# A fused attention and gMLP block: the first loads held one behind another, `wo` loaded earlier, and a new instruction order

## The chip, the cores and the metric

One core of a Trainium2 chip runs the kernel. The time is device microseconds of that core, the median of several executions. One further execution is taken by the hardware profiler; its own time is given beside its span, since a profiled execution is a little longer than the others. The engines are called PE (TensorE, matmul), DVE (VectorE), ACT (ScalarE), POOL (GpSimd) and SP (SyncE, which here only issues transfers).

## The reference

Two blocks with a residual each, on x of 2048 tokens by 512 channels (one batch, bf16).

```python
def _layernorm(x, axis=-1, eps=1e-05):
    m = jnp.mean(x, axis=axis, keepdims=True)
    v = jnp.var(x, axis=axis, keepdims=True)
    return (x - m) / jnp.sqrt(v + eps)

def _A_ref(x, wqkv, wo):                      # linear attention, 32 heads of 16
    qkv = (x @ wqkv).reshape(B, S, 3, H, Dh).transpose(2, 0, 3, 1, 4)
    q, k, v = qkv[0], qkv[1], qkv[2]
    phi = lambda t: jnp.where(t > 0, t + 1, jnp.exp(t)) + 1e-06
    pq, pk = phi(q), phi(k)
    kv = jnp.einsum('bhsd,bhse->bhde', pk, v)
    z = jnp.einsum('bhsd->bhd', pk)
    num = jnp.einsum('bhqd,bhde->bhqe', pq, kv)
    den = jnp.einsum('bhqd,bhd->bhq', pq, z)[..., None] + 1e-06
    return (num / den).transpose(0, 2, 1, 3).reshape(B, S, D) @ wo

def _B_ref(x, w_in, w_sp, b_sp, w_out):       # gMLP, 2 * 896 hidden channels
    z = gelu(x @ w_in)
    z1, z2 = z[..., :Fh], _layernorm(z[..., Fh:])
    g = jnp.einsum('ts,bsf->btf', w_sp, z2) + b_sp[None, :, None]
    return (z1 * g) @ w_out

h = x + _A_ref(_layernorm(x), A_wqkv, A_wo)
out = h + _B_ref(_layernorm(h), B_w_in, B_w_sp, B_b_sp, B_w_out)
```

## The kernel before

Tokens are cut into 16 tiles of 128. The kernel records 853 operations, each with the memory that it reads and writes, through `g.add` (line 106); helpers such as `matmuls` (394), `act` (409 to 423), `dve`, `pool`, `dma` (432) and `dma_t` (a transposing transfer, 435) do so, which is why most rows of the profile carry a helper's line. The order in which the operations are issued is written into the kernel as one packed list, `ORDER` (line 16). `schedule` (144) unpacks it and gives every engine its part of the list in that order; `emit` (163) puts a semaphore wait before an operation wherever it needs something from another engine or from a transfer. Each engine works through its list strictly in order. The estimates `cost` and `lat` of an operation serve the planner's start times, which in the kernel itself only sort an operation's waits.

Stages, in the order of the work of PE:

- **Head.** x is loaded as four single tiles (0 and 2 by SP, 1 and 3 by ACT) and six pairs. The K part of `wqkv` comes in two halves, `wk0` (SP) and `wk2` (ACT), the Q part as `wq`. The pairs are held by SP until tile 0 has landed (`behind`, which adds a dependency, line 481). A warm-up of 42 small matmuls (593) runs while x is on its way. Per tile: `bn_stats` and `bn_aggr` (510, 511) on DVE, the reciprocal root on ACT or POOL (516 to 529; tile 1's moments on ACT and POOL, 534 to 550), the norm (555 on DVE, or ACT), and the transpose to channels by tokens, `xnT`: for tiles 0 to 5 on PE (569) with an eviction by ACT, for the others by a transposing transfer of SP.
- **K and Q.** Per tile four matmuls with K (`psum<-wqkv,xnT`), the map phi (`e` on ACT; 581 and 586 on DVE), and four matmuls that sum pk and xn into four banks (649): the sum over tokens of x's norm times pk, from which kv follows with V's weights. The Q products (`psum<-xnT,wqkv`) stand between them.
- **Joint.** The four sums are copied to `ct`, `wv` is applied (714), the result is masked by heads (`kvm`, 718), multiplied with `wo` and copied to `m` (four products, ACT evictions). So q times m is the attention's output. The denominators (745) go through a log and an exp on ACT to `rcp`, and SP spreads them over partitions (`r<-rcp`, 736); DVE scales pqT with them (758).
- **h.** Per tile four matmuls `psum<-m,pqT`, h by DVE (770), its moments by ACT (`sh`) and POOL (542 to 550), the norm `hn`, and a transposing transfer to `hnT`.
- **gMLP.** Two products with `w_in`: `win2` (796, 799; z2, per tile) and `win1` (`psum<-hnT,win`; z1T, per 512 tokens); z2's norm; the product with `w_sp`, which SP loads with transposing transfers (`wsp`); the gate (864, 865); the product with `w_out` (`wout`), the sum with h (855) and the output.

The loads behind the head are all issued by SP, in the order of the packed list: after the ten xnT transposes come win1, wout, wv, two wsp, win2, a wsp and wo, then the transfers of r and, between them, those of hnT.

Of the kernel before, what the change touches and what calls it, by code (L numbers as in the profile page):

```python
# [8 lines left out]
ACT = mybir.ActivationFunctionType  # L9
ALU = mybir.AluOpType  # L10

P = 128
GRAN = 16
EARLY = 1
SEM_NS = 45.0
ORDER = "c-jTQ13(x66a>(_`&;u?tD)6uwc1+qs)en!Ev*`Bwr$(CZQHhO+qSLuGQbJW$b`(uf~;^wHn_nN8Q}tVc)$~32thG~!W%gO5QbDpiDXEN<VXz%2tM#dF62fIc%eAL;fE3^g}i8hMreq}$c{YlM+8bE9}1u(@*@(3P!Iu#LNv;wA}XLTDj^U>5QHXZie^Ye5}Knjs-Y;VpgMxl0x^g~RkT74)I=@RQCGA?Yjj38bU}CYKri$}U-UyfVo?U8k$|ySirT1yaj1(iD2sAvgSM!L`WS%T=!14Rgu_^jC0K^`=z#G^hY6U3<(P;xNRJgrfmK+EshEuZ7>;2Wh}9T@wHSoK7>Q9hfR5;dX_$f;n2wp4g@c%nd02oWIErI9juSYA*%*SMSc7#qiPLzF7kGlYs;6hDucug#4cLf<ScGlZj!oE%Ihc#x*n=I|iCs90GuVrL*pDsPip#iyb2yI+xPgnfgsZrTYq*YAc#SuBiCegb+qi?fxQ}FffaG-GTcqPdq-O@c!y`P#4}8aae85L!=4X7uSNz34{KOZ0Ln@|VYNlisW+j-GY4{6%%t&WC(uvvVPB*$T6Z5bz!|1{yEXHv9vjl%5fMRh*Ffa2lKMSxR$v-d#GKfVP%#tj{(u`yj<5-r}8P5=wqX)ColeJigp<K*njAm`tU@V)nD|66`i@1adEYCWu$)#+`R&31{?7`K{NpHr`hrZ0kp6tfWtiZag$BL}PL?*EpmvK4ka|LsAGRx3cLpYpO*?<jMnN!%ETeyZpIf6~th`F_uxipM^s={i_BY%x#Z}wpuwq-lEXJ7W?DE8-Qc3@LB<}~J2KIK<I70@=0;aC<{Ax&iw?dBeKWM>ZI0Pf{<1}IQL3RY2tDnwx#%uejWfh?wQ6<35xXa-B_G$U0?XBeeel~%OMC_yob(_!9byvphb@35RM^EJ!s3Xk#)uktasb0%kT9LIAucW@5paw5-i9`|uS7jP}t@f`2+9@q0cH*h2G^DW=;J$Lc|5Aqr}@en6*J}0n&8fqac=n0>)qAKYDA95v+@fk1hIIr^rKhQ^w)L2c_RL#^}E!0x2)LL!SR_)YY9n?{s^qYzL!_WM}ul&m-rB!96Qx$#WbDrck{^Ke>B1C=XMc&{|{@_o(;7fkuDJD~LImlhvRaLu~LMe5Nm-vg-lwKL+C=Yomhf*oEBriEBqrBy!>dK_d%A!}yDwDI)D5qSNO*K?Y)8(eV>ZyL}rGc8EL7Jr@>Z~qWsjeEX{+g^Q8m7S-sj(WW5gMme8lX8EuRfZl_3EbX>aDe!sZr{oxtgz<s;vc@s(Bi%2^yn`nytlJrw!Vqjhdt-TB^-js4ZHf)mo&jTBdDUt`*v@9Xg^t+N*s!s{J~kV>+mvI;7(|r}Mg?UAm~<I;m4Stuwlzo4Tdjx~wa@s%v_ycY379dZN3!r~CS-WcEqP?VG+Rm8Gy(dal=cp_lru_xdac`=Ouut6%!65BjH+_C~O*_FI3H+A<qWW|qd%nxmyNCrfWx%+=g1qdk?od02MKW*O{(oXy2DnWyD2FDqgJ=4ZZ^$MRbN%VoLE-wIlw6|%e*Y#|nEK^A7-meYJJ!Ae<KD`%xG(u!NSm9X*_W3g7oqAbGVtfE!2L`$-VI-zIEXT|K23foy-S5Z5xXuG45R>9(}vi%1tWsrd"


class _Op:
# [13 lines left out]
class _Prog:  # L33
# [219 lines left out]
def bass_sequential_preLN__linear_attn_block__mixer_gmlp__prompt_kernel(  # L253
# [11 lines left out]
    _, S, D = A_x.shape  # L265
# [4 lines left out]
    NT, KD, KF = S // P, D // P, FH // P  # L270
# [7 lines left out]
    g = _Prog(nc)  # L278
# [37 lines left out]
    TB, SB = HT * GW * 2, HT * P * 2  # L316
# [26 lines left out]
    m = g.sbuf("m", o_m, [KD, D], BF16)  # L343
# [43 lines left out]
    def pair(b):  # L387
        return psum[:, b:b + 2, :]
# [42 lines left out]
    def dma(eng, out_ap, in_ap, name, issue=100.0, lat=2500.0, **k):  # L431
        return g.add(eng, lambda q: q.dma_start(out_ap, in_ap), [in_ap], [out_ap], cost=issue, lat=lat, dma=name, **k)  # L432
# [36 lines left out]
    wq = A_wqkv.rearrange("(c p) f -> p c f", p=P)  # L469
    queue = {"SP": [], "ACT": []}  # L470

    def load(eng, dst, src, nm, lat, issue=500.0):
        return dma(eng, dst, src.rearrange("(c p) f -> p c f", p=P), nm, lat=lat, issue=issue)

    def first_load(eng, dst, src, nm, lat, behind=None):
        q = queue[eng]
        op = load(eng, dst, src, nm, lat)
        op.bias = 1e6
        if q:
            op.soft.add(q[-1].i)  # L480
        if behind is not None:
            op.deps.add(behind.i)
        q.append(op)
        return op

    def load_x(eng, n, w, lat, behind=None):
        return first_load(eng, x[:, n:n + w, :], x_d[n * P:(n + w) * P, :], f"x{n}", lat, behind)

    x0 = load_x("SP", 0, 1, 2150)
    load_x("ACT", 1, 1, 2250)  # L490
    load_x("SP", 2, 1, 2500)
    load_x("ACT", 3, 1, 2500)
    for eng, c in (("SP", 0), ("ACT", 2)):
        first_load(eng, wqkv[:, c:c + 2, D:2 * D], A_wqkv[c * P:(c + 2) * P, D:2 * D], f"wk{c}", 3600)
    for n, lat in ((4, 2400), (6, 2600), (8, 2800), (10, 3000), (12, 3200), (14, 3400)):
        load_x("SP", n, 2, lat, x0)
    first_load("SP", wqkv[:, :, 0:D], A_wqkv[:, 0:D], "wq", 4600)
    exp_table = g.add("ACT", lambda ac: ac.preload_act_table_set("natural_log_exp_and_others"), [], [], cost=1300)
    exp_table.soft.add(queue["ACT"][-1].i)
    exps = []  # L500
# [101 lines left out]
    def next_pair():  # L602
        pc[0] += 1
        return PAIRS[pc[0] % 2]
# [83 lines left out]
    qs = [(tg, c) for tg in range(NG) for c in range(0, KD, 2)]  # L688
# [7 lines left out]
    for dst, src, nm in ((wqkv[:, :, 2 * D:3 * D], A_wqkv[:, 2 * D:3 * D], "wv"), (wo, A_wo, "wo"),  # L696
                         (win2, B_w_in[:, FH:F], "win2"), (win1, B_w_in[:, 0:FH], "win1"),
                         (wout, B_w_out, "wout")):
        late = load("SP", dst, src, nm, 2000, issue=src.shape[0] * src.shape[1] * 2 / 350)
        late.soft.add(g.last.i)  # L700


# [18 lines left out]
    for c in range(KD):  # L721
        b = CB[1 - c % 2]
# [15 lines left out]
    for tg in range(NG):  # L738
# [12 lines left out]
        if tg not in MERGE:  # L751
# [38 lines left out]
    for n in range(NT):  # L790
        b = next_pair()
# [11 lines left out]
        src = pair(b).rearrange("p a b -> p (a b)")[:, 0:FH]  # L803
        s = st3[:, n, :]
# [145 lines left out]
```

## Time and profile before

| | us |
|---|---|
| median of 7 executions | 236.38 (236.24 to 238.67) |
| profiled execution, its own time | 237.69 |
| its span, first to last instruction | 236.0 |
| PE busy | 228.7 (97%) |
| DVE busy | 147.4 (62%) |
| ACT busy | 97.5 (41%) |
| POOL busy | 46.1 (20%) |
| transfers | 23.67 MB, mean 100 GB/s |

The mean granted clock of PE over the span is 0.993. A row of the profile names the line, the engine, the operation and what it writes and reads; the times of the queries count from the start of the span. A wait is put down to what ended it last. The rows of a queue (SPq, ACTq) are the issuing of transfers, not the transfers themselves: how long one took is given as the time from issue to landing. The chain goes back from the last instruction and names at each step what released it.

### The profile page before, as it was taken

To read this page: it belongs to the slowest core of one execution; us is meant where nothing else is said; L and a number is where in the kernel's file an instruction comes from. 1 tells how busy PE (TensorE), PEld (TensorE's weight loads), DVE (VectorE), ACT (ScalarE), POOL (GpSimd) and SP (SyncE) were. 2 spreads that over 40 slices of the span, in tenths; PEclk is the share of its full clock that TensorE was granted. 3 is DMA by queue.
4 is the path that set the end of the run, shared out by engine and by line. 5 is a ranking of instruction groups with operands and counts; after the bars stand their busy time and mean duration, and the time that the engine had idled before them with its cause. 6 is when DMAs were issued, how large, how long until landed. Compare 5 with 4: busy or idle time off the path is not lost.

```text
span 236.0 us, 3061 instructions
## 1 busy us (share of the span) xinstructions
PE 228.7 (97%) x1141; PEld 106.0 (45%) x1141; DVE 147.4 (62%) x275; ACT 97.5 (41%) x172; POOL 46.1 (20%) x134
## 2 busy tenths in 40 slices
PE   7899999997999999999999999999999999999995
PEld 6444444452434444454444444444444444444452
DVE  3799765645897430723699796686665018967373
ACT  5576664486999777669761000210001000010000
POOL 3443220000456442226881000000000000000000
PEclk9799999999999999999999999999999999999999
DMA  6982317999344332369999970000000000002044
GB/s 193 292 182 46 74 26 218 261 256 262 89 74 107 67 67 47 67 154 187 139 226 246 198 171 0 0 0 0 3 0 0 0 0 3 0 0 68 0 155 137
DMA packets 58863, 23.67 MB, mean 100 GB/s; under 512 B 48480, under 2 KB 58720, under 8 KB 58848
## 3 DMA queue, kind: packets, MB, share of 16 engines
q1 hardware_dynamic: 58144, 22.88, 43.3%
q10 hardware_dynamic: 704, 0.59, 0.8%
q8 instruction: 9, 0.15, 0.3%
q14 instruction: 6, 0.05, 0.1%
HBM read 7.47 MB, written 2.10 MB: 41 GB/s over the span
## 4 chain that ended last, share of the span: by engine, by line
PE 79%; SPq 6%; DMA 5%; ACT 3%; DVE 3%; POOL 2%; issue 1%
PE psum L402 66%; PE psum L796 5%; SPq L435 4%; PE psum L649 4%; PE psum L799 4%; DMA wo<-in_A_wo_dram 3%; DMA x<-in_A_x_dram 1%; DMA r<-rcp 1%; ACT e L421 1%; DVE h L770 1%; SPq L432 1%; ACT m L421 1%; POOL st L536 1%; DVE pqT L758 1%; POOL rs L550 1%
## 5 line engine op out<-in xcount | busy, mean ns | idle before, releaser
L402 PE MATMUL psum<-wsp,z 128*128 128x512 bf16 x208 | 46.9, 379 | 0.0
L421 ACT ACTIVATE psum<-psum 128x512 f32<-128x512 f32 x12 | 7.0, 583 | 85.3 <-DVE u L864 50.5
L402 PEld LDWEIGHTS psum<-wsp,z 128*128 128x128 bf16 x208 | 20.3, 98 | 24.6 <-DVE z L555 0.2
L864 DVE TENSOR_TENSOR u<-psum,bsp 128x512 bf16<-128x512 f32 x16 | 11.1, 691 | 27.4 <-PE psum L402 27.3
L402 PE MATMUL psum<-hnT,win 128*128 128x512 bf16 x112 | 26.0, 379 | 0.0
L402 PE MATMUL psum<-wout,z1T 128*128 128x512 bf16 (+1 forms) x119 | 25.2, 367 | 0.0
L402 PE MATMUL psum<-t,s 128*128 128x512 bf16 x96 | 22.2, 379 | 0.0
L421 ACT ACTIVATE e<-psum 128x1024 bf16<-128x1024 f32 (+1 forms) x18 | 16.7, 927 | 12.4 <-PE psum L402 12.1
L421 ACT ACTIVATE z1T<-psum 128x512 bf16<-128x512 f32 x28 | 16.2, 595 | 4.8 <-PE psum L402 4.8
L402 PEld LDWEIGHTS psum<-wout,z1T 128*128 128x128 bf16 x119 | 11.6, 98 | 12.8 <-DVE z1T L865 0.5
L421 ACT ACTIVATE z<-psum 128x896 bf16<-128x896 f32 x16 | 14.6, 913 | 5.0 <-PE psum L799 4.9
L402 PE MATMUL psum<-wqkv,xnT 128*128 128x512 bf16 x64 | 16.5, 409 | 0.0
L796 PE MATMUL psum<-win,hnT 128*128 128x512 bf16 x64 | 16.4, 379 | 0.0
L402 PEld LDWEIGHTS psum<-hnT,win 128*128 128x128 bf16 x112 | 10.1, 98 | 13.3 <-ACT z1T L421 3.5
L649 PE MATMUL psum<-pk,xn 128*128 128x512 bf16 x64 | 15.3, 380 | 0.0
L402 PE MATMUL psum<-m,pqT 128*128 128x512 bf16 x64 | 15.0, 380 | 0.3 <-DVE h L770 0.2
L402 PE MATMUL psum<-xnT,wqkv 128*128 128x512 bf16 x64 | 15.3, 379 | 0.0
L855 DVE TENSOR_TENSOR h<-psum,h 128x512 bf16<-128x512 f32 (+1 forms) x17 | 10.8, 657 | 6.9 <-PE psum L402 6.9
L402 PEld LDWEIGHTS psum<-t,s 128*128 128x128 bf16 x96 | 9.4, 98 | 11.3
L812 DVE BATCH_NORM_STATS2 st<-z 128x6 f32<-128x512 bf16 x9 | 6.2, 687 | 12.0 <-ACT z L421 11.9
L799 PE MATMUL psum<-win,hnT 128*128 128x384 bf16 x64 | 13.0, 326 | 0.0
L770 DVE SCALAR_TENSOR_TENSOR h<-psum,x 128x512 bf16<-128x512 f32 x16 | 10.8, 687 | 3.1 <-PE psum L402 3.0
(99 smaller groups left out, 307.4 us busy)
## 6 DMA issues: line engine op xcount, KB each, us to landing
r<-rcp SPq DMA_DIRECT2D x16, 128.0 KB, 2.8
out_dram<-h SPq DMA_DIRECT2D x15, 128.0 KB, 1.8
win<-in_B_w_in_dram SPq DMA_DIRECT2D x2, 896.0 KB, 5.5
x<-in_A_x_dram SPq DMA_DIRECT2D x6, 256.0 KB, 5.7
wqkv<-in_A_wqkv_dram SPq DMA_DIRECT2D x2, 512.0 KB, 8.2
wout<-in_B_w_out_dram SPq DMA_DIRECT2D x1, 896.0 KB, 8.5
wo<-in_A_wo_dram SPq DMA_DIRECT2D x1, 512.0 KB, 6.6
bsp<-in_B_b_sp_dram SPq DMA_DIRECT2D x1, 512.0 KB, 4.4
```

The costliest lines, as they stand in the source:

```text
L402: inst = pe.matmul(out_ap, lhsT=a, rhs=b, start=start and i == 0, stop=stop and i == len(pairs) - 1, **kw)
L421: return g.add("ACT", lambda ac: ac.activation(out_ap, in_ap, func, **kw), [in_ap, *extra], [out_ap] + ([accum] if accum is not None else []),
L432: return g.add(eng, lambda q: q.dma_start(out_ap, in_ap), [in_ap], [out_ap], cost=issue, lat=lat, dma=name, **k)
L435: return g.add("SP", lambda q: q.dma_start_transpose(out_ap, in_ap), [in_ap], [out_ap], cost=issue, lat=lat, dma=name, **k)
L536: pool(lambda p: p.tensor_scalar(ve, s[:, 2:3], s[:, 1:2], EPS_LN, op0=ALU.add, op1=ALU.add), [s[:, 1:3]], [ve], 240)
L649: inst = pe.matmul(bank(CB[c]), lhsT=xn[:, i, c * P:(c + 1) * P], rhs=pk[:, i, :], start=i == 0, stop=i == NT - 1)
L770: dve(lambda v, n=n, b=b, s=s: v.scalar_tensor_tensor(h[:, n, :], bank(b), 1.0, x[:, n, :], op0=ALU.mult, op1=ALU.add, accum_out=s[:, 0:1] ...
L796: pe.matmul(bank(b), lhsT=hnT[:, c, n * P:(n + 1) * P], rhs=win2[:, c, 0:GW], start=c == 0, stop=c == KD - 1)
L799: inst = pe.matmul(bank(b + 1, F2), lhsT=hnT[:, c, n * P:(n + 1) * P], rhs=win2[:, c, GW:FH], start=c == 0, stop=c == KD - 1)
L812: dve(lambda v, n=n, s=s: v.bn_stats(s[:, 0:6], z2[:, n, 0:GW]), [z2[:, n, 0:GW]], [s[:, 0:6]], GW)
L855: dve(lambda v, o=o, b=b: v.tensor_tensor(o, bank(b, w), o, ALU.add), [bank(b, w), o], [o], w, ps=True)
L864: dve(lambda v: v.tensor_tensor(t, bank(b), add, ALU.add), [bank(b), add], [t], GW, ps=True)
```

## The change

Three edits. The first pair of tiles, 4 and 5, is loaded with no wait. Pair 6 waits for tile 0, pair 8 for tile 2, and pairs 10, 12 and 14 for `wk0`. The estimates of latencies for the planner are set anew, among them 5500 in place of 2000 for the late weights. The packed list is a new one of the same 853 operations. On SP, the loads behind the head come as follows: nine xnT transposes, wo, the tenth, win2, wout, win1, a wsp, wv, a wsp, the transfers of r. Of the later wsp transposes of 8 blocks, two stand among the hnT transposes of tiles 4 to 7, five ahead of the last four hnT, and the rest behind. On PE, the products of the head are laced differently (transposes and K products of single tiles in turn), the second denominator product comes ahead of the product with wv, and a Q product comes between the two halves of the products with wo. The order of DVE, ACT and POOL follows.

```diff
-ORDER = "c-jTQ13(x66a>...
+ORDER = "c-jTQ13(x66a>...
...
     x0 = load_x("SP", 0, 1, 2150)
     load_x("ACT", 1, 1, 2250)
-    load_x("SP", 2, 1, 2500)
+    x2 = load_x("SP", 2, 1, 2500)
     load_x("ACT", 3, 1, 2500)
-    for eng, c in (("SP", 0), ("ACT", 2)):
-        first_load(eng, wqkv[:, c:c + 2, D:2 * D], A_wqkv[c * P:(c + 2) * P, D:2 * D], f"wk{c}", 3600)
-    for n, lat in ((4, 2400), (6, 2600), (8, 2800), (10, 3000), (12, 3200), (14, 3400)):
-        load_x("SP", n, 2, lat, x0)
-    first_load("SP", wqkv[:, :, 0:D], A_wqkv[:, 0:D], "wq", 4600)
+    wk = [first_load(eng, wqkv[:, c:c + 2, D:2 * D], A_wqkv[c * P:(c + 2) * P, D:2 * D], f"wk{c}", 3500)
+          for eng, c in (("SP", 0), ("ACT", 2))]
+    for n, lat, behind in ((4, 3900, None), (6, 3500, x0), (8, 3600, x2), (10, 3300, wk[0]), (12, 3500, wk[0]),
+                           (14, 3700, wk[0])):
+        load_x("SP", n, 2, lat, behind)
+    first_load("SP", wqkv[:, :, 0:D], A_wqkv[:, 0:D], "wq", 4500)
...
-        late = load("SP", dst, src, nm, 2000, issue=src.shape[0] * src.shape[1] * 2 / 350)
+        late = load("SP", dst, src, nm, 5500, issue=src.shape[0] * src.shape[1] * 2 / 350)
```

The instruction order of SP around the late loads, before and after:

```
before                                   after
xnT transposes x10                       xnT transposes x9
win1                                     wo
wout                                     xnT transpose x1
wv                                       win2
wsp x2                                   wout
win2                                     win1
wsp                                      wsp
wo                                       wv
r transfers x12                          wsp
                                         r transfers x12
```

More of the change, by code (lines that the diff above doesn't have):

```diff
@@ L15 @@
 SEM_NS = 45.0
-ORDER = "c-jTQ13(x66a>(_`&;u?tD)6uwc1+qs)en!Ev*`Bwr$(CZQHhO+qSLuGQbJW$b`(uf~;^wHn_nN8Q}tVc)$~32thG~!W%gO5QbDpiDXEN<VXz%2tM#dF62fIc%eAL;fE3^g}i8hMreq}$c{YlM+8bE9}1u(@*@(3P!Iu#LNv;wA}XLTDj^U>5QHXZie^Ye5}Knjs-Y;VpgMxl0x^g~RkT74)I=@RQCGA?Yjj38bU}CYKri$}U-UyfVo?U8k$|ySirT1yaj1(iD2sAvgSM!L`WS%T=!14Rgu_^jC0K^`=z#G^hY6U3<(P;xNRJgrfmK+EshEuZ7>;2Wh}9T@wHSoK7>Q9hfR5;dX_$f;n2wp4g@c%nd02oWIErI9juSYA*%*SMSc7#qiPLzF7kGlYs;6hDucug#4cLf<ScGlZj!oE%Ihc#x*n=I|iCs90GuVrL*pDsPip#iyb2yI+xPgnfgsZrTYq*YAc#SuBiCegb+qi?fxQ}FffaG-GTcqPdq-O@c!y`P#4}8aae85L!=4X7uSNz34{KOZ0Ln@|VYNlisW+j-GY4{6%%t&WC(uvvVPB*$T6Z5bz!|1{yEXHv9vjl%5fMRh*Ffa2lKMSxR$v-d#GKfVP%#tj{(u`yj<5-r}8P5=wqX)ColeJigp<K*njAm`tU@V)nD|66`i@1adEYCWu$)#+`R&31{?7`K{NpHr`hrZ0kp6tfWtiZag$BL}PL?*EpmvK4ka|LsAGRx3cLpYpO*?<jMnN!%ETeyZpIf6~th`F_uxipM^s={i_BY%x#Z}wpuwq-lEXJ7W?DE8-Qc3@LB<}~J2KIK<I70@=0;aC<{Ax&iw?dBeKWM>ZI0Pf{<1}IQL3RY2tDnwx#%uejWfh?wQ6<35xXa-B_G$U0?XBeeel~%OMC_yob(_!9byvphb@35RM^EJ!s3Xk#)uktasb0%kT9LIAucW@5paw5-i9`|uS7jP}t@f`2+9@q0cH*h2G^DW=;J$Lc|5Aqr}@en6*J}0n&8fqac=n0>)qAKYDA95v+@fk1hIIr^rKhQ^w)L2c_RL#^}E!0x2)LL!SR_)YY9n?{s^qYzL!_WM}ul&m-rB!96Qx$#WbDrck{^Ke>B1C=XMc&{|{@_o(;7fkuDJD~LImlhvRaLu~LMe5Nm-vg-lwKL+C=Yomhf*oEBriEBqrBy!>dK_d%A!}yDwDI)D5qSNO*K?Y)8(eV>ZyL}rGc8EL7Jr@>Z~qWsjeEX{+g^Q8m7S-sj(WW5gMme8lX8EuRfZl_3EbX>aDe!sZr{oxtgz<s;vc@s(Bi%2^yn`nytlJrw!Vqjhdt-TB^-js4ZHf)mo&jTBdDUt`*v@9Xg^t+N*s!s{J~kV>+mvI;7(|r}Mg?UAm~<I;m4Stuwlzo4Tdjx~wa@s%v_ycY379dZN3!r~CS-WcEqP?VG+Rm8Gy(dal=cp_lru_xdac`=Ouut6%!65BjH+_C~O*_FI3H+A<qWW|qd%nxmyNCrfWx%+=g1qdk?od02MKW*O{(oXy2DnWyD2FDqgJ=4ZZ^$MRbN%VoLE-wIlw6|%e*Y#|nEK^A7-meYJJ!Ae<KD`%xG(u!NSm9X*_W3g7oqAbGVtfE!2L`$-VI-zIEXT|K23foy-S5Z5xXuG45R>9(}vi%1tWsrd"
@@ new lines @@
+ORDER = "c-jTQ13(x66a>(_`&;u?tD)6uwc1+qs)en!Ev*`Bwr$(CZQHhO+qSLuGQbJW$b`(uf~@d>CmfLxE^tQ}LQo8$00=`eq(myDMshen@J0^ggcp3^i(JSJKNLqeN}xRQq9RJ60xF>a8X-IKz#kDPfP5&4D3nGa<VPe5A{qfGjK*k)L?odJnxYw+qX;S^27#!CAXGt7R7DF^M@`f~Ewn-$x}q~;(FNU52Cm2kH`Gx}v_@@=MLZHv2X!$HqcH}Hu@p<N48bUia%h9L=#CWVfu87v@tA-~n26;_i!@k)RY-@GNRQs=gTCm8dZ>^77=U(Yj}AD1gE)l4n2O05h(Q>PBRGm<IF8{MhSeB>kr;)wIE87Lf{y5f8JLdwn1`8IfD>4QbvTWuIEiO?f#;~JCzyrV7=oeLfc032Mc9b#*oIBmj5(N#-PnU2*oj>@i!<1Zeb|pJ*orH-jB_}T3%G%cxP+^?iEFryS9pWhc!^uMi#xc7+jxLvypQB`U^+fTdS>8Tyu%|r#&>+gd;GvBe85+HMrQuQU;M-ue8X?lQ);GUDyCo-W~CDy>CB8w%QXCjKk#E77G@a3=}#ACViA_0E8XbMY|P7i%+CTW$T$`w7(lT&BS^+GkU=cUU>d8lENih4LztcA=)q8Waxt5+23s<LIq1dmtjUrr#nOyq6r)+2br{R8T+LQ&&K~rkFJoASIqA(sT*5V6%FS%eE!@fqtjM~o$NFr*N^HnPCec^BnM-@vf=#%VJz1H#S(Ulih?AK|>)4G`IGnjPghM%kZP=FW*q+PSft}f%z34ALHDwjnS7SC%HRe}d^=2RTWk2@k0Pf{J?&lyDP+{d$L5*Y~711;XC`i*8sG<s1s6tdsGZ>~}EUu|M%y32M2#>OaN~$9Vaxgow3rBG@4{!`;au#QEERS&;xAQnpa1PgV0}pZ>=W;nuasf|sJSTD<OR2OX6|E@6Dn@ZCqce<Gf^PFN%jyoVu$;>4Dqr(4-|z{4^ADf$E>H0+&+!@?s*xJ2iJEEx=W`(^@gDE<IydqLAMhdH@*UsvJRfldFYqFt@e&X5FaHsG&XwH37ktT`yvbW!#a-OQ52QY_k}Bvk6ID@3N~<rdtglR`WJ<3La#V6T=o`ONswQ_iDWg&-rBdk!v&%!C${{cPWNI~2bG49<TB?;=tBu;Ko!YB|I;xYZ%SD-#S<cF$ta`;yOe1f(Dw}f3<fbaBrK+l-n)=1b>Z_jWr(Wu>l^Uq&8l>8qp&^>3&KjmJ>Z;)yp(&cC!5XQl8ml=Ps&QJQRT{6knx}5+uHNdQ0h+JHnyIxKr3LDv(VDF>nxKiAq$OIfb=siSTBxPkq-ENu&Dx?x+Ny0@t`*v@9Xg^t+N*s!s{J~kgF2?2I;7(|sZ%<wGuoxyI;Zoxpv$_VtGcKgx~W^brrWx!d%CYjdaNh<sJD8j4@zdAl-#~3g?&>hd!^@ktv7n1m-?=!dauuNu%G&?ulk{XN@>3Y`>h8`ZD}pD(bActrLjMfnWeW3=48&6#azwBGFm2cx9nEL@>_rvFgNqCtmbLiEQfiSpZQuI3$|PqV!6%V@>-~cSwRc5AoI4I=3@y~+{#)x3%3#$W3g7o%3C2TWu-0BA}r1-S|v-gC`+>II-xttXU}w4MeUM`*+Uh!v#MYvE#9K7vi%3_(U5@"
```

## The prediction

> **What bounds the kernel now.** I read the busy times first, then TensorE's (PE's) waits, then the chain, and last the time lines around each place where PE lost time. The page's first part:
>
> ```profile
> PE 228.7 (97%) x1141; PEld 106.0 (45%) x1141; DVE 147.4 (62%) x275; ACT 97.5 (41%) x172; POOL 46.1 (20%) x134
> ```
>
> PE is busy for all but 7.3 us of the span of 236.0 us, and both kernels issue the same matmuls, so a reordering can win only idle time or half-rate time, and it loses by making new idle time. The waits of PE say where the idle time lies:
>
> ```profile
> PE psum L569 <- DVE xn L555: 1.5, 3, 1.0
> PE psum L402 <- DMA wo<-in_A_wo_dram: 1.4, 1, 1.4
> PE psum L593 <- POOL warm L439: 1.0, 1, 1.0
> ```
>
> (Total us, times, longest.) Three losses: the first tiles' norm (1.5), `wo` (1.4), and the constant that the warm-up reads (1.0, before any input has landed); the other two rows are 0.2 each. The chain and PE's time line around the third:
>
> ```profile
> 48.79 6.61 DMA wo<-in_A_wo_dram
> 55.40 0.14 issue
> 55.54 0.39 PE psum L402
> ```
> ```profile
> 55.54 0.59 PE L402 MATMUL psum<-wo,kvm 128*128 128x512 bf16 x2 [1.38 <-DMA wo<-in_A_wo_dram]
> 56.06 0.40 PE L745 MATMUL psum<-pqT,zc 128*32 128x512 bf16 x4
> 56.60 0.88 PE L402 MATMUL psum<-wo,kvm 128*128 128x512 bf16 x2
> 57.32 1.89 PE L402 MATMUL psum<-xnT,wqkv 128*128 128x512 bf16 x8
> 59.04 1.24 PE L402 MATMUL psum<-m,pqT 128*128 128x512 bf16 x5
> ```
>
> `wo` is the last load of SP's queue, issued at 48.79, landed at 55.40. The table by stretch shows the rest:
>
> ```profile
> 7.93:11.35 3.42, 3.42 (x12) 1.45 (x12) 3.02 (x9) 1.74 (x4) 1.24 (x3) 0.50 0.97 292
> ...
> 50.00:59.00 9.00, 7.38 (x52) 3.23 (x49) 4.23 (x7) 6.72 (x12) 0.00 (x0) 1.00 1.01 265
> 59.00:67.00 8.00, 7.58 (x38) 3.25 (x38) 6.85 (x18) 7.56 (x15) 4.45 (x11) 1.00 0.37 82
> 67.00:77.00 10.00, 9.89 (x49) 4.38 (x48) 8.36 (x23) 9.86 (x25) 5.41 (x15) 1.00 0.52 93
> ```
>
> (Columns: length; busy PE, weight loads, DVE, ACT, POOL; granted clock; DMA share; GB/s.) One stretch of 3.4 us in the head runs at half clock: eight matmuls step by 0.43 us there against 0.22 after it, 1.6 us lost while PE counts as busy. From 59 to 77 ACT and DVE are nearly full as well, so time gained ahead of 59 may be given back there.
>
> **Part 1, wo first.** SP's order behind the xnT transposes was win1, wout, wv, wsp, wsp, win2, wsp, wo. It becomes wo (ahead of the last xnT transpose), then that transpose, win2, wout, win1, wsp, wv, wsp. wo is issued at about 30.6 (the transpose that now stands last but one is ready near 29: its norm on ACT moves up ahead of two exps). It costs 0.58 us of SP; the last transpose, whose norm ends near 33.4, goes out near 33.5 (35.19 before), so SP waits there anyway and wo is hidden. wo lands near 35 and is out of the question.
>
> What follows on PE is then set by kvm. The q product and r product (50.07 to 51.3), the wv product of 16 matmuls (1.06, 51.3 to 52.4), a q product (0.86, to 53.2), which covers DVE's kvm (0.69, done at 53.1). Two wo products (0.43), q (0.86) to 54.5. The first two m evictions on ACT (0.6 each) follow its rcp, which ends at 53.74, so they end near 54.9; two wo products to 55.1; the r product 0.4; two q products 1.73 to 57.2. ACT has e (1.03) and two m (1.1) to do after 54.8, to 56.9. So the first m,pqT product starts near 57.2 where it started at 59.04: -1.8 us. ACT's own hole, 53.74 to 55.95, goes with it, so its full stretch starts earlier too.
>
> Given back: the products 4 and 5 wait for PSUM evictions, which DVE (0.69 each) makes in line with the r scalings: 0.45 and 0.2. r lands sooner: it was issued at 51.57 and took 4.1 to 4.7 us behind wo, against 2.8 as the median of all r transfers; the first scaling, at 57.02 before, can start near 55.4. Products 8 and 14 wait 0.4 each for the scalings of the third and fourth groups, where before gaps of 0.2 to 0.4 stood at like places. I count 0.6 lost of the 1.8: **-1.2 us** after 77.
>
> **Part 2, wv late.** wv moves behind 2.7 MB of other weights. Before, win1 landed 5.1 us after its issue, wout 4.0 us later (at 45.6), wv at 47.0 (9.3 us after its issue). SP's own time line has the order, and two wsp issues held 4.6 and 3.9 us by the full queue:
>
> ```profile
> 36.50 0.58 SPq L432 DMA_DIRECT2D win<-in_B_w_in_dram  x1
> 37.13 0.50 SPq L432 DMA_DIRECT2D wout<-in_B_w_out_dram  x1
> 37.67 0.56 SPq L432 DMA_DIRECT2D wqkv<-in_A_wqkv_dram  x1
> 38.28 8.56 SPq L435 DMA_TRANSPOSE wsp<-in_B_w_sp_dram  x2
> 46.89 0.58 SPq L432 DMA_DIRECT2D win<-in_B_w_in_dram  x1
> ```
>
> Now: win2 issued near 34.75, landed 39.9; wout 43.9; win1 47.2 to 47.9; wsp 0.9; wv 1.4 more: 49.5 to 50.2. Needed at 51.3. The row bounds it from above by the transfer that stood behind two wsp before (win2, 52.8, a stall of 1.5), from below by nothing (0). I take 0, since bytes and start are counted, and keep 1.5 for the range.
>
> **Part 3, the head.** x4 goes out at 2.2 instead of 3.56. It stands in SP's queue behind wk0, and it landed at 7.39 before, with wk0 at 6.68 and wk2 (ACT's queue) at 6.89, while the DMA engines moved 302 GB/s from 4.5 to 7.9 at a share of 0.93: it is rate-bound, and lands at 7.0 to 7.4. [...] By the row, where x4's first pieces had landed at 6.30, ahead of the end of both weights, they shared the engines already, and the cost is 0. I take 0 and keep 0.4: the first k product can't start before 7.3, when its xnT eviction ends.
>
> Wait for wk0: the load of x10 now holds SP from 4.6 to 6.7, with x12, x14, wq, the first wsp and all xnT transposes behind it. They go out from 6.7 to 8.8 instead of 5.0 to 7.0. The queue doesn't run dry: x8 landed only at 10.1. The wsp issue, held until 13.44 by the queue before (6.38 us; 1.3 to 2.9 where free), ends near 13.5 again, at worst at 8.8 + 6.4 = 15.2. The first xnT transpose waits for its norm on ACT, now near 14.7 (two evictions and an exp moved ahead), and lands near 17.2 to 18; its product comes at 18.9.
>
> PE's order: transpose 0, 2, k0, transpose 1, k2, and so on. k0 starts near 7.3 (8.16 before), half of it ahead of the half-rate stretch; transpose 1 waits for tile 1's norm, which is 0.7 later (8.5), since one stats of x4 (0.69) and an ACT step (0.28) stand ahead. Then 0.43 us a matmul to 11.35, k3 to 13.0, the rest set by DVE's pk: the k product of tile 6 starts near 18.9 against 19.07, and the product after it has no 0.2 us hole: **-0.3 us**, between -0.9 and +0.8.
>
> [...] Row: 1.91 of 3.41 us busy from 4.52 to 7.93, and half rate in the next. By the row the stretch stays (0). [...]
>
> **Part 4, from 77 to the end.** wsp transposes move between the hnT transposes: two by 80, then five ahead of the last four hnT. Two cost 2.6 us of SP; hnT 5 is then issued near 80 and lands near 82.5, needed at 85. The five: 1.31 us each where the queue was empty (98.9 to 101.6), 1.64 as the mean of nine back to back; so 6.6 to 8.2 us from 89, four hnT of 1.27, and 2.5 to land: 103 to 105, needed near 107.9. No cost. Nothing in the tail moves the last product or its output (2.5 us behind PE's end). 0, with +0.5 for small holes, since PE had none from 75.4 to 233.
>
> **Sum:** -1.2 - 0.3 = -1.5: span 234.5. The profiled execution took 237.69 (span 236.0 and 1.7 around it), so it would take 236.2; the runs' median is 236.38, and the same step from it gives **234.9 us**. From no change a measurement of this kernel tells about 0.5%, or 1.2 us.
>
> **Rivals.** (a) ACT and DVE take the gain: they are 9.9 and 8.4 busy of 10 us from 67 to 77. For it: that row; against: ACT's hole at 54 closes too. Time 236.2. (b) wv is late by 1.5: the same wait under another name; 236.4. For it the 8.5 and 9.3 us that wout and wv took; against it the start, 1.75 us sooner. (c) Slower: the five wsp ahead of the last four hnT are held by a full queue as from 38.28 to 46.84 (3.9 and 4.6 us each) instead of 1.3 to 1.6. It decides from 2.2 us each; at 2.9 it cancels the gain and costs 2 more: 238.4. Against it: wsp are alone in the queue there. [...]
>
> **Numbers.** Forecast 0.52, (a) 0.20, (b) 0.10, (c) 0.09, (d) 0.09. The forecast's own range is 233.7 to 235.6; faster by over 0.5% means below 235.2. The forecast gives 0.46 faster and 0.06 same; (a) 0.04, 0.14, 0.02; (b) 0, 0.07, 0.03; (c) all slower; (d) 0.01, 0.04, 0.04. Sum: 0.51, 0.31, 0.18. The range of 8 in 10 is 233.5 to 237.7.
>
> **What would show it.** Right: no wait of PE for wo, m,pqT starting near 57.3, wv landing before 51. Wrong: PE waiting for wv at L715, for xt6 near 19, for hnT near 85 or 107, or a half-rate row past 11.4.

## The result, and the profile after

The changed kernel takes 235.34 us (median of 22 executions, 234.60 to 236.22) against 236.55 us of the kernel before (57 executions beside it, 235.41 to 239.47). The ratio is 0.9938, 95% interval 0.9921 to 0.9955: about 1.5 us faster. The plain medians lie 1.21 us apart (0.9949), inside that interval, so the size of the gain is known to about 0.4 us. Its profiled execution took 234.94 us, with a span of 233.2 us, and so lies under the median of its kernel; that of the kernel before (237.69) lay above, as executions with a half-rate stretch do (medians of 237.6 to 238.3 us in the experiments, against 236.4 to 236.6 without).

The first part of its page has the same work as before, and PE is idle for 6.0 us in place of 7.3:

```profile
PE 227.2 (97%) x1141; PEld 105.8 (45%) x1141; DVE 147.8 (63%) x275; ACT 97.4 (42%) x172; POOL 44.2 (19%) x134
```

The waits of PE (total us, times, longest). The wait for `wo` is gone; one for the K weights, which did not exist, has come:

```profile
PE psum L570 <- DVE xn L556: 1.4, 4, 0.5
PE psum L594 <- POOL warm L439: 1.0, 1, 1.0
PE psum L402 <- DMA wqkv<-in_A_wqkv_dram: 0.6, 1, 0.6
PE psum L402 <- DVE h L771: 0.2, 1, 0.2
```

PE's time line around the products with `wo` (start, length, what, how many matmuls). The first starts at 52.64, straight after a Q product, and the first `m,pqT` product (attention's output, the first product of the stage h) at 56.60 (59.04 before):

```profile
50.79 1.07 PE L715 MATMUL psum<-ct,wqkv 128*128 128x128 bf16 x16
51.69 1.03 PE L402 MATMUL psum<-xnT,wqkv 128*128 128x512 bf16 x4
52.64 0.60 PE L402 MATMUL psum<-wo,kvm 128*128 128x512 bf16 x2
53.08 1.03 PE L402 MATMUL psum<-xnT,wqkv 128*128 128x512 bf16 x4
53.95 0.65 PE L402 MATMUL psum<-wo,kvm 128*128 128x512 bf16 x2
54.53 0.40 PE L746 MATMUL psum<-pqT,zc 128*32 128x512 bf16 x4
54.86 1.90 PE L402 MATMUL psum<-xnT,wqkv 128*128 128x512 bf16 x8
56.60 1.67 PE L402 MATMUL psum<-m,pqT 128*128 128x512 bf16 x7
```

The table by stretch (length; busy PE, weight loads, DVE, ACT, POOL; granted clock; DMA share; GB/s):

```profile
9.32:12.74 3.42, 3.19 (x20) 1.43 (x20) 3.42 (x12) 2.40 (x5) 1.64 (x4) 1.00 0.93 282
50.00:57.00 7.00, 7.00 (x49) 3.13 (x48) 3.97 (x6) 6.94 (x11) 0.00 (x0) 1.00 0.55 131
57.00:65.00 8.00, 7.72 (x37) 2.90 (x36) 7.42 (x19) 6.93 (x16) 4.19 (x11) 1.00 0.42 100
65.00:75.00 10.00, 10.00 (x52) 4.88 (x50) 8.12 (x23) 9.60 (x21) 4.58 (x13) 1.00 0.67 119
```

Two things are to be seen. From 50 to 57 PE is busy throughout, where before it was busy for 7.38 of 9 us. And the clock is full in the head, where the profile before has a stretch at half rate. That second difference isn't what the change won: a second profile of the kernel before (experiment 8) has the full clock as well, and its last matmul starts at 232.12, not 233.12. So before and after are compared below by profiles with the full clock, and the table gives for each kernel where PE stands at four places.

| profile | clock in the head | first Q product | first `wo` product | first `m,pqT` | last matmul | `wo` landed |
|---|---|---|---|---|---|---|
| before | half, 3.4 us | 24.44 | 55.54 | 59.04 | 233.12 | 55.40 |
| before, second profile | full | 23.83 | 54.34 | 57.84 | 232.12 | 54.20 |
| changed | full | 23.70 | 52.64 | 56.60 | 230.35 | 33.73 |
| before, `wo` first | full | 23.45 | 53.01 | 56.52 | 230.70 | 39.57 |
| before, new x waits | full | 24.27 | 54.59 | 58.09 | 232.17 | 54.45 |
| changed, `wo` last | full | 24.03 | 52.96 | 56.92 | 230.67 | 50.41 |
| changed, old late loads | half, 3.4 us | 24.30 | 53.23 | 57.19 | 230.87 | 51.83 |
| changed, `wo` behind rcp | full | 23.57 | 55.36 | 60.56 | 234.24 | 55.23 |
| changed, old x waits | full | 23.19 | 52.12 | 56.08 | 229.83 | 33.73 |
| changed, again | full | 23.82 | 52.76 | 56.71 | 230.46 | 34.09 |
| changed, x4 behind x0 | full | 23.36 | 52.30 | 56.26 | 230.00 | 33.68 |

Differences of columns are steadier than the columns. From the first Q product to the first `m,pqT` product it is 34.60 and 34.01 us in the two profiles of before, 33.83 in the kernel before with the new x waits, 33.07 with `wo` first, and 32.89 or 32.90 in every kernel with the changed order but the one that holds `wo` back on purpose. From there to the last matmul it is 174.07 to 174.28 in the old order (174.19 with `wo` first), and 173.68 to 173.76 in the changed one. In this pair of profiles at the full clock the change is thus worth 0.13 us in the head, 1.11 between the first Q product and the first `m,pqT`, and 0.53 behind it: 1.77, the difference of 232.12 and 230.35. The medians of the executions with a mean clock of 0.999 or 1.000 give less: 235.08 us (15 of the 22) against 236.53 (56 of the kernel before beside the experiments), 1.4 to 1.5 us.

### The profile page after: what moved, and what is told of

Read it like the earlier page. It is cut to its first block, busy times and chain, and to the rows that moved or that the text cites. A ratio compares the mean times of both kernels' runs of the same rounds, so it can differ in the third digit from the quotient of the medians.

```text
span 233.2 us, 3051 instructions
## 1 busy us (share of the span) xinstructions
PE 227.2 (97%) x1141; PEld 105.8 (45%) x1141; DVE 147.8 (63%) x275; ACT 97.4 (42%) x172; POOL 44.2 (19%) x134
## 4 chain that ended last, share of the span: by engine, by line
PE 88%; DMA 4%; DVE 3%; ACT 2%; SPq 1%; POOL 1%; issue 0%; ACTq 0%; DVEq 0%
PE psum L402 70%; PE psum L797 6%; PE psum L650 6%; PE psum L800 4%; DMA x<-in_A_x_dram 3%; DMA r<-rcp 1%; DVE st L511 1%; SPq L737 1%; SPq L432 1%; DVE h L771 1%; ACT pqT L421 0%; PE psum L671 0%; DVE xn L556 0%; PE psum L680 0%; PE psum L746 0%
## 5 line engine op out<-in xcount | busy, mean ns | idle before, releaser
L402 PE MATMUL psum<-wqkv,xnT 128*128 128x512 bf16 x64 | 15.3, 379 | 0.6 <-DMA wqkv<-in_A_wqkv_dram 0.6
L556 DVE TENSOR_SCALAR hn<-h,st,rs 128x512 bf16<-128x512 bf16 x16 | 6.3, 408 | 12.6 <-POOL rs L547 12.3
L511 DVE BATCH_NORM_STATS2 st<-x 128x6 f32<-128x512 bf16 x15 | 9.8, 678 | 4.9 <-DMA x<-in_A_x_dram 4.9
```

Source lines behind the costliest of these rows:

```text
L402: inst = pe.matmul(out_ap, lhsT=a, rhs=b, start=start and i == 0, stop=stop and i == len(pairs) - 1, **kw)
L511: dve(lambda v: v.bn_stats(s[:, 0:6], src[:, n, :]), [src[:, n, :]], [s[:, 0:6]], D)
L556: return dve(lambda v: v.tensor_scalar(dst, src, mean, rst, op0=ALU.subtract, op1=ALU.mult), [src, mean, rst], [dst], w + 460, acc=4)
```

## Experiments

The theory on trial (called A in the expectations): the gain is the end of the wait for `wo`. The rivals: it comes from the new head, from PE's new order as such, or ACT and DVE take part of it back. Each experiment names the kernel it starts from; the ratio is always to the kernel before on the same chip.

**1. `wo` first, and nothing else (in the kernel before).** 230 is the load of `wo`, 204 the last xnT transpose.

```diff
         ids = np.frombuffer(zlib.decompress(base64.b85decode(ORDER)), np.uint16).tolist()
+        ids.remove(230)
+        ids.insert(ids.index(204) + 1, 230)
```

> The kernel before, with one step moved: wo's load goes out behind the last xnT transpose, ahead of win1, wout, wv and the two wsp transposes. Nothing else differs. Theory A (the gain is the end of the wait for wo): the first m,pqT product starts 1.5 to 1.8 us earlier than in the kernel before and little of it is lost later: time down by 1.2 to 1.8 us, a ratio of 0.992 to 0.995. Rival B (ACT and DVE, nearly full from 59 to 77, take the gain): the first m,pqT product earlier by as much, but the end earlier by less than 0.4 us, ratio 0.998 to 1.000. Rival C (the gain of the changed kernel comes from its head and the new order of the engines): no wait for wo any more, but another in its place behind it, since PE's order is still the old one; ratio 0.997 to 1.002.

Measured: 235.41 us, ratio 0.9934 (0.9906 to 0.9962). The first `wo` product starts at 53.01, with no wait:

```profile
53.01 0.59 PE L404 MATMUL psum<-wo,kvm 128*128 128x512 bf16 x2
```

That is 1.33 us ahead of the second profile of before; the first `m,pqT` and the last matmul follow by 1.32 and 1.42. Of this, 0.38 is there at the first Q product already, which no edit explains (the head is the same in both), so the moved load is worth 1.0 us in this pair: 0.94 up to the first `m,pqT` and 0.09 behind it. By the ratio, one moved load gives the gain of the whole change, within the intervals. That flatters it a little: none of its 8 executions shows the half clock, and 5 of the 20 of the kernel before beside it do. Among those at the full clock the medians are 235.41 and 236.44: 1.0 us, where the whole change has 1.4 to 1.5. Rival B falls: nothing of the gain is taken back. Rival C falls for this order, since the head and PE's order are the old ones.

**2. `wo` last (in the changed kernel).** 229 is `wv`, 607 the second wsp transpose.

```diff
+        ids.remove(607)
+        ids.insert(ids.index(229) + 1, 607)
+        ids.remove(230)
+        ids.insert(ids.index(607) + 1, 230)
```

> The changed kernel, with wo's load moved back: behind win2, wout, win1, the wsp transpose, wv and the second wsp transpose, just ahead of the r transfers. All else as in the changed kernel, the head and the order of PE, DVE and ACT too. Theory A: PE waits for wo again ahead of the wo products, for 1.5 us or more (wo would be issued near 46 and land near 50 to 54; it is needed at 52.6): the time comes back to the kernel before's or above, ratio 1.000 to 1.01. Rival C (head and order make the gain): ratio stays at 0.994 to 0.996.

Measured: 235.25 us, ratio 0.9930 (0.9894 to 0.9967). My theory's number failed. `wo` landed at 50.41, well before PE came to it at 52.96, so the edit brought no wait back. It stood one wsp transpose short of the place that it had before, and the queue ahead of it had started sooner: `wo` was issued at 45.78, against 48.15 and 48.79 in the two profiles of before.

**3. All late loads in the old order (in the changed kernel).** The numbers stand for win1, wout, `wv`, wsp, wsp, win2, wsp and `wo`, put behind the last xnT transpose (202).

```diff
+        late = [232, 233, 229, 606, 607, 231, 608, 230]
+        ids = [i for i in ids if i not in late]
+        k = ids.index(202) + 1
+        ids[k:k] = late
```

> The changed kernel with all late loads back in the order of the kernel before, behind the last xnT transpose: win1, wout, wv, two wsp transposes, win2, a third wsp transpose, wo, then the r transfers. PE, DVE, ACT, POOL and the head stay as changed. Theory A (what was gained at wo is its place behind win2 and three wsp transposes): wo is issued near 48 and lands at 53.5 to 54.5; PE needs it at 52.6 and waits 1 to 2 us for it; the time rises by 1 to 1.8 us over the changed kernel, ratio to the kernel before 0.998 to 1.001. Rival C (PE's new order has other work for that time, so the place of wo is of no account): ratio 0.992 to 0.995.

Measured: 235.21 us, ratio 0.9941 (0.9914 to 0.9969). The theory's number failed again, and rival C's (0.992 to 0.995) held. SP's time line in this kernel:

```profile
34.39 0.58 SPq L436 DMA_DIRECT2D win<-in_B_w_in_dram  x1
...
36.17 7.27 SPq L439 DMA_TRANSPOSE wsp<-in_B_w_sp_dram  x2
43.48 0.58 SPq L436 DMA_DIRECT2D win<-in_B_w_in_dram  x1
44.11 2.07 SPq L439 DMA_TRANSPOSE wsp<-in_B_w_sp_dram  x1
46.23 0.57 SPq L436 DMA_DIRECT2D wo<-in_A_wo_dram  x1
```

The same list of loads starts 1.5 to 2.1 us sooner than in the two profiles of before (35.89 and 36.50), since the last xnT transpose is ready sooner in the new order, and the two wsp transposes hold SP for 7.27 us in place of 8.54 and 8.56. `wo` is issued at 46.23 (48.79 before) and lands at 51.83, 1.4 us ahead of its use at 53.23, where before it came after its use. So the wait had two cures in this change, and each suffices: `wo` ahead of the others, or all of them 1.5 to 2 us sooner, which the new order brings. Rival C is right that far, though not by other work on PE: `wo` was in time. The place of `wo` is what frees the old order (experiment 1); in the new order it is a reserve.

**4. `wo` held back until the first rcp (in the changed kernel).** As experiment 2, with `wo` behind operation 262, the first rcp, and dependent on it.

```diff
+        ids.remove(607)
+        ids.insert(ids.index(229) + 1, 607)
+        ids.remove(230)
+        ids.insert(ids.index(262) + 1, 230)
+        self.ops[230].deps.add(262)
```

> The changed kernel with wo's load held back on purpose: it goes out behind the two wsp transposes and only when the first rcp is done, near 51, just ahead of the r transfers. Theory A (a late wo costs one for one once it lands after PE wants it, near 53): wo lands at 53.5 to 55, PE waits 0.8 to 2.2 us for it, the first m,pqT product moves from 56.6 to 57.5 to 59, and the end moves by as much: 0.8 to 2.4 us over the changed kernel, ratio 0.997 to 1.004. Rival J (the stage behind is bound by the r transfers and the scalings on DVE, so a wait for wo is taken up again): the end moves by less than 0.4 us, ratio 0.992 to 0.995.

Measured: 239.45 us, ratio 1.0108 (1.0065 to 1.0151): 4.1 us above the changed kernel, more than either expected. PE's time line:

```profile
51.56 1.03 PE L407 MATMUL psum<-xnT,wqkv 128*128 128x512 bf16 x4
55.36 1.01 PE L407 MATMUL psum<-wo,kvm 128*128 128x512 bf16 x2 [2.78 <-DMA wo<-in_A_wo_dram]
56.17 1.91 PE L407 MATMUL psum<-xnT,wqkv 128*128 128x512 bf16 x4
57.88 0.68 PE L407 MATMUL psum<-wo,kvm 128*128 128x512 bf16 x2
58.49 0.40 PE L751 MATMUL psum<-pqT,zc 128*32 128x512 bf16 x4
58.82 1.90 PE L407 MATMUL psum<-xnT,wqkv 128*128 128x512 bf16 x8
60.56 3.62 PE L407 MATMUL psum<-m,pqT 128*128 128x512 bf16 x16
```

The wait is 2.78 us, yet the first `m,pqT` comes 4.09 us later after the first Q product (36.99 against 32.90). The table by stretch has the rest (columns as above):

```profile
47.81:51.22 3.41, 3.32 (x29) 1.51 (x29) 0.67 (x4) 3.28 (x7) 0.00 (x0) 1.00 0.06 12
51.22:54.63 3.41, 1.37 (x14) 0.64 (x10) 2.25 (x3) 1.72 (x3) 0.00 (x0) 1.00 0.79 214
54.63:58.04 3.41, 2.68 (x7) 1.02 (x8) 1.29 (x2) 1.09 (x2) 0.00 (x0) 0.50 0.89 248
58.04:61.46 3.42, 3.42 (x20) 1.33 (x18) 0.74 (x2) 3.34 (x5) 0.00 (x0) 1.00 0.01 2
```

A stretch with 1.37 us of work is followed by one at half clock, in which four Q matmuls take 1.91 us in place of 1.03. From the Q product to the first `wo` product it is 3.80 us in place of 0.95, 2.85 more by the wait; from there to the first `m,pqT` 5.20 in place of 3.96, 1.24 more at the half clock. Together they are the 4.09, and all of it reaches the end (173.68 from the first `m,pqT` to the last matmul, as in the other kernels with this order): rival J falls. So a late `wo` costs at least its own wait. That the half clock comes with it is not a rule: one of the six executions has a mean clock of 1.000 and took 238.65 us, so its time, 3.5 us above the changed kernel, was lost without it.

**5. and 6. The old x waits in the changed kernel; the new x waits in the kernel before.** The lines are those of 5; 6 puts the new waits into the kernel before, with that kernel's own estimates of latency.

```diff
-    for n, lat, behind in ((4, 3900, None), (6, 3500, x0), (8, 3600, x2), (10, 3300, wk[0]), (12, 3500, wk[0]),
-                           (14, 3700, wk[0])):
+    for n, lat, behind in ((4, 3900, x0), (6, 3500, x0), (8, 3600, x0), (10, 3300, x0), (12, 3500, x0),
+                           (14, 3700, x0)):
```

> The changed kernel, order and all, with the old waits of the x loads: every pair from x4 to x14 waits for x0 alone, as in the kernel before. Theory A1 (the early x4 takes its share of the DMA engines from the two K weights, and the later loads gain nothing by being held): wk0 and wk2 land 0.4 to 0.9 us sooner (near 6.7 to 6.9 as in the kernel before), the first k product starts near 7.4, the time falls by 0.3 to 0.6 us against the changed kernel: ratio to the kernel before 0.9915 to 0.9925. Rival D (the waits are what makes the new head faster: with all x loads let go at x0 they crowd each other again): the k product of tile 6 comes back to near 19.1 and the ratio rises to 0.996 to 0.998. Rival E (the head's loads make no difference to the end, as DVE sets the k products): within 0.1% of the changed kernel.

> The kernel before, its order of the engines and all, with the new waits of the x loads alone: x4 and x5 with no wait, x6 behind x0, x8 behind x2, x10 to x14 behind wk0. Theory A1 (these waits cost): the K weights land 0.5 to 0.9 us later, the first k product starts near 8.2 to 8.8 as its order has both transposes ahead of it, the end comes 0 to 0.6 us later: ratio 1.000 to 1.0025. Rival D (the waits make the gain of the head): the k product of tile 6 starts 0.5 us earlier, ratio 0.997 to 0.998.

Measured: the changed kernel with the old waits 234.40 us, ratio 0.9895 (0.9859 to 0.9930); the kernel before with the new waits 237.27 us, ratio 1.0013 (0.9982 to 1.0044). Theory A1 has the sign right in both; in the changed kernel the gain is larger than it had (0.9915 to 0.9925), and in the kernel before the interval holds no change as well, but not rival D's 0.997 to 0.998. What A1 had first, the weights landing sooner, didn't come in the profile of the changed kernel with the old waits: `wk0` landed at 7.36. The kernel was run once more, beside the changed kernel itself:

> The changed kernel with the old waits (all pairs from x4 on wait for x0 alone), a second time. If the first result holds: ratio 0.9885 to 0.9905. If it was spread: 0.992 to 0.9945.

> The changed kernel, unchanged, on the same chip and in the same rounds as the kernel with the old waits, for a direct comparison. Ratio 0.992 to 0.9955. If the new waits of the x loads cost what the first comparison gave (0.4%), it stands 0.5 to 1 us above the changed kernel with the old waits; if that was the spread of chips and runs, within 0.3 us of it.

Measured: 234.37 us, 0.9891 (0.9855 to 0.9927), and 235.33 us, 0.9945 (0.9918 to 0.9972). So the new waits cost 0.96 us in the medians, 0.4 to 0.5% (0.75 us among the executions at the full clock, 235.12 and 234.37); in the profiles with the full clock 0.5 to 0.6 of it is there at the first Q product (23.19 against 23.70 and 23.82) and no more comes behind it. What they do shows in the stretch from 7 to 9 us. The changed kernel, again:

```profile
7.00:9.00 2.00, 1.40 (x8) 0.53 (x8) 1.03 (x3) 1.23 (x3) 0.35 (x1) 1.00 0.59 182
```

and with the old waits:

```profile
7.00:9.00 2.00, 1.75 (x13) 0.82 (x14) 1.46 (x3) 1.46 (x3) 0.32 (x1) 1.00 1.01 289
```

With x10 held until `wk0` has landed, the DMA engines have less to move: a share of 0.59 and 182 GB/s against 1.01 and 289. Over the profiles the share in this stretch is 0.59 to 0.81 with the new waits (six profiles) and 0.87 to 1.07 with the old (six); with the hold behind `wk0` alone it is 0.83 (one, of experiment 7). The weights come later too: with x4 let go at once, `wk0` lands at 7.07 to 7.73 and x4 itself at 7.95 to 8.47 (six profiles); with x4 behind x0, at 6.51 to 6.68 and 7.29 to 7.51 in five profiles. In two others (7.36 and 7.27, x4 at 8.16 and 8.03) they landed late with x4 behind x0 as well, so the same loads move by as much with nothing changed, and a single pair of profiles would not have settled it.

That the early x4 takes a share from both weights, as A1 has it, the traces bear out at most in part. They have sixteen updates of a load's semaphore, one after another as its pieces land (those of `wk0` from 4.75 to 7.25 us in the first profile of the changed kernel). The median of the sixteen for `wk0` is no later with x4 let go at once (5.24 to 6.33 us in the six profiles) than with x4 behind x0 (5.17 to 6.07 in the seven); for `wk2` it is perhaps a little later (5.67 to 6.72 and 5.59 to 6.27). What is late is the last pieces: in the changed kernel, again, 13 of the 16 of `wk0` are in by 5.40 us and the last comes at 7.13. Why a few pieces stay behind is open.

**7. Which of the two waits?** x4 behind x0 but the hold behind `wk0` kept; and the reverse.

```diff
-    for n, lat, behind in ((4, 3900, None), (6, 3500, x0), (8, 3600, x2), (10, 3300, wk[0]), (12, 3500, wk[0]),
+    for n, lat, behind in ((4, 3900, x0), (6, 3500, x0), (8, 3600, x2), (10, 3300, wk[0]), (12, 3500, wk[0]),
```

> The changed kernel with one wait back: x4 and x5 wait for x0; x6 behind x0, x8 behind x2 and x10 to x14 behind wk0 stay. Theory F (the early x4 is what costs: it takes its share of the DMA engines while wk0 and wk2 come, and all later pieces shift): the time is that of the changed kernel with all old waits, ratio 0.989 to 0.991. Theory G (holding x10 to x14, wq and the first wsp transpose behind wk0 is what costs, as the xnT transposes of tiles 6 and 7 go out later): ratio stays at 0.993 to 0.994.

The reverse leaves x4 with no wait and puts x6 to x14 behind x0.

> The changed kernel with x4 and x5 loaded with no wait as in it, but all later pairs waiting for x0 alone, as in the kernel before. Theory F: ratio 0.993 to 0.994, as the changed kernel. Theory G: ratio 0.989 to 0.991, as with all old waits.

Measured: 234.75 us, 0.9922 (0.9893 to 0.9950), and 235.63 us, 0.9936 (0.9908 to 0.9964). One execution of the second took 617.46 us; its profile is of that one and tells nothing here. The order is that of theory F, but the first of the two doesn't reach the 0.9893 of the old waits, and the intervals overlap. The order may also be that of the clock alone: 1 of 8 executions of the first shows the half clock and 5 of 11 of the second, and among the others the medians are the same, 234.70 and 234.76 us. Both lie between 235.1 with both new waits and 234.4 with neither. In the one usable profile (`x4 behind x0` in the table) the first Q product starts at 23.36, 0.17 behind the old waits and 0.34 and 0.46 ahead of the new. That both parts cost something fits best; their shares stay open.

**8. The kernel before, again.** No edit.

> The kernel before, unchanged, for a second profile and to see what no change measures. If the clock is full through the head in this one, then, by the kernel before with the new waits (first m,pqT product at 58.1, last matmul at 232.2), the half-rate stretch in the first profile was worth about 1.3 us: first m,pqT product near 57.5 to 57.9, last matmul near 231.6 to 232. Ratio 0.998 to 1.002.

Measured: 236.77 us, ratio 1.0001 (0.9973 to 1.0028). This profile has the full clock, and its wait for `wo` is shorter:

```profile
54.34 0.59 PE L402 MATMUL psum<-wo,kvm 128*128 128x512 bf16 x2 [0.79 <-DMA wo<-in_A_wo_dram]
```

The first `m,pqT` is at 57.84 and the last matmul at 232.12, about as expected. `wo` landed at 54.20 against 55.40 in the first profile: half of this, 0.64, is a later issue (48.15 and 48.79), the other half, 0.56, a longer way (6.05 and 6.61). Two executions of one kernel differ by 0.6 us in this one wait (0.79 and 1.38).

**9. DVE's norm of tile 1 ahead of x4's statistics (with the old x waits).**

```diff
+        ids.remove(43)
+        ids.insert(ids.index(78), 43)
```

> The changed kernel with the old waits, and with one step moved on DVE: the norm of tile 1 ahead of the first bn_stats of tile 4, so that it no longer stands behind a wait for x4's landing. Theory H (x4's landing holds up DVE, and PE through it): the transpose of tile 1 starts near 7.7 in place of 9.3, and the K product of tile 1 follows that of tile 0 without the 0.3 us hole; since DVE then reaches pk a little later or at the same time, the end comes 0 to 0.4 us earlier: ratio 0.988 to 0.990. Rival I (DVE's sum of work up to the first pk sets the pace, and that is the same): within 0.1% of the changed kernel with the old waits.

Measured: 234.03 us, 0.9888 (0.9851 to 0.9924), against 234.37 and 0.9891: no difference that can be told. Its profile has a half-rate stretch in the head, so the place of single products says little; the transpose of tile 1 started at 9.24 all the same, since PE's order has the K product of tile 0 ahead of it, which started at 7.58. The question isn't settled. This kernel and that of experiment 5 are the fastest here, and both beat the changed kernel.

## Why the prediction was right, and where it was right by luck

The sum, -1.5 us, was measured as -1.5 (236.55 times 1 - 0.9938; the plain medians give -1.2, and 235.34 us where 234.9 was forecast). Its parts were not all so.

- **Part 1, up to the first `m,pqT`.** The chain by kvm, ACT's evictions and the Q products was right: 57.2 less 24.44 of the first Q product is 32.8, and 32.90 was measured. The size, -1.8, was taken from one execution, though, in which `wo` came late by more than in the other: against the two profiles of before it is -1.70 and -1.11. That the wait for `wo` was what cost is shown for the old order (experiment 1), and what such a wait would cost in the new one by experiment 4. But moving `wo` wasn't needed in the new order (3), which starts all late loads sooner. The prediction had that earlier start (1.75 us, in rival (b)), but used it for `wv` alone.
- **Part 1, given back 0.6.** This step failed. Two holes came about as large as written: 0.60 and 0.43 us from one matmul to the next ahead of the products 4 and 6, counted from 0 (4 and 5 were forecast), 0.6 together beyond the usual step of 0.22. Those at products 8 and 14 did not, and the holes that the first profile of before has between 65 and 76 us (steps of 0.59, 0.60, 0.38 and 0.44) went. The reading that failed is that full engines make PE wait: ACT and DVE are about as full as before (9.60 and 8.12 of 10 us from 65 to 75), yet PE has no hole there. 0.3 to 0.6 us was gained behind the first `m,pqT`, not lost. Rival (a), which built on the same two busy shares, falls with it. The step with `wo` first and the old order gained only 0.1 there, so this gain is the new order's.
- **Part 2, `wv` at no cost.** Right. SP's time line after:

```profile
32.56 1.21 SPq L435 DMA_TRANSPOSE xnT<-xn  x1
33.82 0.58 SPq L432 DMA_DIRECT2D win<-in_B_w_in_dram  x1
34.44 0.51 SPq L432 DMA_DIRECT2D wout<-in_B_w_out_dram  x1
34.99 0.56 SPq L432 DMA_DIRECT2D win<-in_B_w_in_dram  x1
35.59 4.69 SPq L435 DMA_TRANSPOSE wsp<-in_B_w_sp_dram  x1
40.33 0.58 SPq L432 DMA_DIRECT2D wqkv<-in_A_wqkv_dram  x1
```

  `wv`, issued at 40.33, landed at 48.02 (written: 49.5 to 50.2) and was needed at 50.79. Rival (b) falls.
- **Part 3, the head, -0.3.** About nothing was gained by the change: 0.13 by the first Q product against the second profile of before (0.74 against the first, of which 0.61 is between the two profiles of before themselves). Two steps failed here, "it is rate-bound, and lands at 7.0 to 7.4" and "I take 0": the early x4 landed at 8.21, and both weights came later, `wk0` at 7.25 (6.68 before) and `wk2` at 7.83 (6.89). The first K product started at 7.97, not near 7.3. The chain of the changed kernel begins with x4, and PE's time line has the wait for `wk0` or `wk2`:

```profile
2.18 6.03 DMA x<-in_A_x_dram
8.23 0.69 DVE st L511
```
```profile
7.97 1.02 PE L402 MATMUL psum<-wqkv,xnT 128*128 128x512 bf16 x4 [0.62 <-DMA wqkv<-in_A_wqkv_dram]
9.30 0.40 PE L570 MATMUL psum<-ident,xn 128*128 128x128 bf16 x4 [0.30 <-DVE xn L556]
```

  No run shows the 0.4 that was kept; in its place this pair of profiles shows `wk2` 0.94 later, and those of experiments 5 and 6 show 0.5 to 0.6 us at the first Q product as the cost of the new waits together. The cause is not shown: `wk0`, which stands ahead of x4 in the same queue, was late by 0.57 as well, x4 itself landed 0.82 later than before (8.21 and 7.39), and of `wk0` only the last pieces are late (experiments 5 and 6). And "The queue doesn't run dry" was wrong in effect: from 7 to 9 us the share fell to between 0.59 and 0.81. Against the cost of 0.5 to 0.6 us here stood a gain of the new order in the head that I hadn't separated: at the full clock with the old waits the first Q product starts at 23.19 in the new order, and at 23.45 and 23.83 in the old. That is 0.3 to 0.6 us, though the two profiles of the old order lie 0.4 apart themselves.
- **The half-rate stretch.** "By the row the stretch stays" took what one execution showed for a property of the kernel. In the experiments 14 of 80 executions of the kernel before, the second profile's included, show a mean clock of 0.992 or 0.993, as that profile did, and the others the full one; of the changed kernel, 12 of 34 show it. The forecast was made as a step from the median, so the total took little harm.
- **Part 4 and the rest.** Right: the five wsp took 2.24 us for the first and 1.3 to 1.5 for the others, the last hnT landed at 103.22 (used first at 106.33), and PE had no hole from 75 on. Rival (c) falls, and so does (d), one half-rate stretch more in the head, which was no more than my estimate: in this profile the clock is 1.00 from 9.32 to 12.74, behind the pause of 0.30 us ahead of the transpose of tile 1.

So the total was right by luck, since three errors cancelled: a wait sized by a late execution (0.1 to 0.7 too much), a loss that did not come (0.6, with 0.3 to 0.6 of gain in its place), and a head that won next to nothing (0.13 where 0.3 was forecast), as its new waits cost about what its new order gained. The experiments put the gain together otherwise than the sum. At the full clock the medians are 236.4 to 236.6 us before, 235.4 with `wo` first, 234.3 to 234.4 with the whole new order and the old x waits, and 235.1 with the new waits.

## What to carry to other kernels

Where one load ends a wait, try that move alone before a whole new order is searched: here one moved load gave about 1.0 of the 1.4 to 1.5 us, and in the rest of the change a gain of about 1 us by the new order and a loss of 0.8 to 1 us by the new x waits hid each other. Size a wait on a transfer from more than one profile: that for `wo` moved by 0.6 us with nothing changed. And try loads that are let go early or held back on their own, with the order left as it is: here they cost about as much as the order gained in the head.

## What the runs showed of the hardware

In these profiles, whether a stretch of 3.41 us runs at the half clock goes with how much PE worked in the one before. The stretches are those of the clock's own record. In the first profile of the kernel before it has entries of 3.413 us from 4.52 (full) and from 7.93 (half), and then 225.28 us at the full clock, 66.0 times as long; in that of the changed kernel it has 228.69 us at the full clock from 5.91 on, 67.0 times as long. Where they fall differs between executions: those at half rate begin at 7.43, 7.92, 7.93, 8.19 and 54.63 us. With 1.37 us of busy PE (experiment 4), 1.49 (3), 1.74 (9), 1.80 (the first profile of 5) and 1.91 (the kernel before), a stretch was followed by one at half rate; with 1.84 (changed), 2.04 (changed, again), 2.06 (old x waits, again, and experiment 6), 2.10 (2), 2.20 (7) and more it was not. The two groups overlap (1.91 with, 1.84 without), so the busy time that the profile gives doesn't part them by one figure. The heads of the two kernels lie where they meet (1.91 and 1.84), and each kernel shows the stretch in some executions and not in others (14 of 80 and 12 of 34). And a wait of 2.78 us in the middle of the kernel was followed by one, which added another 1.24 us (experiment 4).

The landing of one load moves between executions with nothing changed: `wo` by 0.56 us from its issue (6.05 and 6.61), and `wk0` by 0.81 us in the changed kernel with the old x waits (landed at 6.55 and 7.36).
